# Second product turned round: w_out stationary, g moving in four 64x64 tiles, and a transpose of the output on VectorE

## Chip, cores, metric

One core of a Trainium2 chip. The metric is the device time of one execution in microseconds (us), on the slowest core (there is only one). "Before" and "changed" name the two kernels.

## The reference

```python
# a short causal convolution over the sequence, softmaxed weights per head, then a two-layer product
out = einsum('hk,bskhg->bshg', softmax(weight), windows_of(x))   # x: 8 x 4096 x 192, 8 heads, 7 taps
h = out.reshape(32768, 192) @ w_in                               # w_in: 192 x 2048
g = maximum(0.01 * h, h)
return g @ w_out                                                 # w_out: 2048 x 192, result fp32
```

Three parts share the work: VectorE does the convolution (y), TensorE the first product (h = y w_in), ScalarE the leaky ReLU on the way from PSUM to SBUF (g), TensorE the second product (g w_out).

## The kernel before

32 blocks of 2 x 512 tokens (two batch rows, index `e`). The first four blocks are worked in half groups of 256 tokens, to get going earlier; the other 28 are whole groups of 512. The second product of a group runs during the next group's first product, in "slots": a slot is the matmuls for one of the 16 pieces of 128 hidden channels.

The contraction of the first product is 192 = 3 x 64, so the array is split into two row tiles of 64 rows, one for each batch row:

```python
def mm1(grp, u):                       # one unit of the first product: 128 hidden channels
    ...
    for c in range(NCH):               # 3 pieces of the contraction
        for e in range(2):             # row tile = batch row
            ps = slice(e * CH, (e + 1) * CH)
            nc.tensor.matmul(out=ph[:, e, i * T : (i + 1) * T], lhsT=w_in_of(f, ps, c),
                             rhs=y[ps, c, t0 : t0 + T], start=(c == 0), stop=(c == NCH - 1))
    nc.scalar.activation(out=g[blk][...], in_=ph, func=Prelu, alpha=0.01)

def mm2_one(rt, m, fc, start, stop):   # second product: g stationary, w_out moves, 192 columns
    ...
    return nc.tensor.matmul(out=po[m], lhsT=g[b][ps, fc, e, s * 128 : (s + 1) * 128],
                            rhs=w_out[ps, fc, :], start=start, stop=stop)
```

The two row tiles each take half of a 128-long piece of the contraction, and the kernel keeps them out of one PSUM bank at the same time. So a pair of outputs is worked in two rounds (row tile 0 on output A and 1 on B, then the other way), with a "seal" between: a small ScalarE or VectorE instruction that waits for the last matmul of the round and is waited for by the first of the next.

```python
def mm2_slot(q):
    ...
    for rt in range(2):
        ins = mm2_one(rt, pair[rt ^ rnd], fc, first and rnd == 0, last and rnd == 1)
        if first and rnd == 1:
            sync(ins, seal, "both row tiles have left these banks")
    if last and rnd == 0:
        seal_round(p, ins)             # evacuates the previous pair's second output
    if last and rnd == 1:
        evac_o(pair[0])                # copy PSUM -> SBUF, 128 x 192, then a store
```

## Time and profile before

| | before |
|---|---|
| time, median of 3 | 692.45 us (691.92 to 692.78) |
| span of the profiled run | 690.8 us |
| TensorE, VectorE, ScalarE busy | 99%, 73%, 74% |
| output packets | 768 B each |

The three groups of the page that the change touches, besides those that the prediction shows. Columns: line, engine, operation, out<-in, sizes, count | busy us, mean ns of one | idle before it:

```profile
L429 PE MATMUL po<-w_out,g 64*128 64x192 bf16 (+1 forms) x8064 | 387.9, 243 | 0.0
L403 PE MATMUL ph<-yt,w_in 64*128 64x512 bf16 (+1 forms) x3456 | 384.1, 352 | 1.5 <-ACT g L410 0.7
...
L476 DVE COPY o_sb<-po 128x192 f32<-128x192 f32 x224 | 80.1, 358 | 163.9 <-PE po L429 156.3
```

The two products cost about the same. TensorE is hardly ever idle, while VectorE's copies wait for it.

### The profile page before, as it was taken

The page shows a single profiled execution, that of the slowest core. Times are in us where ns is not written, and L with a number is a line of the kernel's source. Part 1 is how long each engine was busy: PE and PEld are TensorE (multiplying, and loading weights), DVE is VectorE, ACT ScalarE, POOL GpSimd, SP SyncE. Part 2 cuts the span into 40 slices and gives each one's busy share as a digit, 9 for nine tenths or more (in the row PEclk, how much of TensorE's full clock was granted, in tenths as well). Part 3 has the DMA queues.
Part 4 walks back from the last instruction along what each step waited for, and adds up shares of the span by engine and source line. Part 5 has one row for each costly group of instructions (what it writes and reads, how often), then busy time and mean ns, then how long its engine had stood idle before and what let it go on. Part 6 is the DMA issues. An engine that isn't in the chain of part 4 may idle for free.

```text
span 690.8 us, 25914 instructions
## 1 busy us (share of the span) xinstructions
PE 685.2 (99%) x11708; PEld 584.0 (85%) x11708; DVE 501.6 (73%) x986; ACT 514.4 (74%) x569; POOL 148.0 (21%) x206
## 2 busy tenths in 40 slices
PE   9999999999999999999999999999999999999998
PEld 6999988888888888888888888888888888888887
DVE  5899666777777787777787777777777877777712
ACT  6888898777777777777777777777777777777771
POOL 6822222211222201222202222112222112000000
PEclk9999999999999999999999999999999999999999
DMA  9976656455565545565455566355565455322112
GB/s 151 117 93 94 82 69 84 80 78 70 75 85 82 76 77 75 66 94 82 71 78 71 74 84 88 67 78 75 77 82 80 77 75 66 67 60 59 48 42 64
DMA packets 184159, 53.79 MB, mean 78 GB/s; under 512 B 149104, under 2 KB 183664, under 8 KB 184048
## 3 DMA queue, kind: packets, MB, share of 16 engines
q0 software_dynamic: 99536, 14.76, 30.2%
q1 hardware_dynamic: 84512, 37.38, 22.8%
q8 instruction: 91, 1.49, 0.9%
q14 instruction: 20, 0.16, 0.1%
HBM read 29.88 MB, written 25.17 MB: 80 GB/s over the span
## 4 chain that ended last, share of the span: by engine, by line
PE 98%; ACT 2%; issue 0%; DVE 0%
PE po L429 49%; PE ph L403 47%; ACT g L410 2%; PE acc L212 1%; PE warm L284 1%; PE ptr L149 0%; ACT yt L371 0%; DVE o_sb L476 0%; PE ptr L156 0%; PE wps L320 0%; PE wps_l L320 0%; DVE zero L227 0%; DVE junk L229 0%
## 5 line engine op out<-in xcount | busy, mean ns | idle before, releaser
L410 ACT ACTIVATE g<-ph 128x1024 bf16<-128x1024 f32 x512 | 496.3, 1021 | 155.9 <-PE ph L403 155.4
L193 DVE SCALAR_TENSOR_TENSOR yt<-xt,wk,yt 128x512 bf16<-128x512 bf16 (+1 forms) x630 | 399.5, 691 | 0.2
L429 PEld LDWEIGHTS <-g 64*128 64x128 bf16 (+1 forms) x8064 | 361.9, 94 | 34.4 <-issue 0.2
L429 PE MATMUL po<-w_out,g 64*128 64x192 bf16 (+1 forms) x8064 | 387.9, 243 | 0.0
L403 PE MATMUL ph<-yt,w_in 64*128 64x512 bf16 (+1 forms) x3456 | 384.1, 352 | 1.5 <-ACT g L410 0.7
L403 PEld LDWEIGHTS <-w_in 64*128 64x128 bf16 x3456 | 226.0, 111 | 64.7 <-issue 3.7
L78 POOL DMA_DIRECT2D x_bf<-in_x_dram x180 | 134.6, 772 | 422.6 <-DMA xt<-x_bf 420.1
L476 DVE COPY o_sb<-po 128x192 f32<-128x192 f32 x224 | 80.1, 358 | 163.9 <-PE po L429 156.3
L187 DVE TENSOR_SCALAR yt<-xt,wk 128x512 bf16<-128x512 bf16 (+1 forms) x105 | 36.8, 381 | 12.8 <-DMA xt<-x_bf 12.6
L476 ACT COPY o_sb<-po 128x192 f32<-128x192 f32 x32 | 10.2, 320 | 1.5 <-PE po L429 0.2
L168 DVE COPY xt<-ptr 128x384 bf16<-128x384 bf16 x7 | 2.2, 354 | 6.9 <-PE ptr L156 4.5
L212 PE MATMUL acc<-xt,diag 64*64 64x256 bf16 x84 | 6.7, 327 | 0.0
L212 PEld LDWEIGHTS <-diag 64*64 64x64 bf16 x84 | 5.5, 133 | 1.3 <-DVE wk L366 0.4
L284 PE MATMUL warm<-zero 128*128 128x256 bf16 (+1 forms) x20 | 4.8, 405 | 1.1 <-DVE junk L229 1.1
L127 POOL DMA_DIRECT2D x_half<-in_x_dram x6 | 4.3, 714 | 3.2 <-DMA w_in<-in_moe_w_in_dram 3.2
L284 PEld LDWEIGHTS <-zero 128*128 128x128 bf16 x20 | 2.5, 136 | 2.1 <-DVE junk L229 1.1
L249 POOL DMA_DIRECT2D w_in<-in_moe_w_in_dram x6 | 3.9, 654 | 0.0
L371 ACT ACTIVATE yt<-acc,rsum 128x256 bf16<-128x256 f32 x3 | 1.4, 474 | 2.9 <-PE acc L212 2.9
L345 ACT ACTIVATE diag<-ident,whm 128x64 bf16<-128x64 bf16 x14 | 3.5, 335 | 0.0
L123 POOL DMA_DIRECT2D x_rows<-in_x_dram x4 | 2.9, 733 | 0.2 <-issue 0.2
L133 ACT CAST x_half<-x_nat 128x384 bf16<-128x384 f32 x2 | 1.0, 512 | 1.2 <-DMA x_nat<-in_x_dram 1.1
L290 ACT ACT_TABLE_LOAD x1 | 1.3, 1283 | 0.8 <-PEq L575 0.8
(37 smaller groups left out, 11.9 us busy)
## 6 DMA issues: line engine op xcount, KB each, us to landing
out_dram<-o_sb SPq DMA_DIRECT2D x117, 192.0 KB, 2.1
x_bf<-in_x_dram POOLq DMA_DIRECT2D x180, 64.0 KB, 3.2
out_dram<-o_sb SPq DMA_DIRECT2D x22, 96.0 KB, 1.6
xt<-x_bf SPq DMA_TRANSPOSE x90, 2.5
w_in<-in_moe_w_in_dram POOLq DMA_DIRECT2D x4, 192.0 KB, 5.8
w_in<-in_moe_w_in_dram POOLq DMA_DIRECT2D x2, 384.0 KB, 9.4
w_out<-in_moe_w_out_dram POOLq DMA_DIRECT2D x1, 768.0 KB, 11.2
x_nat<-in_x_dram SPq DMA_DIRECT2D x2, 192.0 KB, 2.6
```

The source lines that it names most:

```text
L78: nc.gpsimd.dma_start(out=t[:, c, :, e, :], in_=src[2 * rp + e, :, :, c * CH : (c + 1) * CH],)
L127: nc.gpsimd.dma_start(out=x_half[q][:, c, :, e, :], in_=rows[:, e, :, c * CH : (c + 1) * CH],)
L187: lambda s=src, d=dst, c=c: nc.vector.tensor_scalar_mul(d, s, wk[:, c, 0:1])
L193: lambda s=src, d=dst, c=c, k=k: nc.vector.scalar_tensor_tensor(out=d, in0=s, scalar=wk[:, c, k : k + 1], in1=d, op0=mybir.AluOpType.mult, ...
L212: lambda k=k, p=p, a=a, e=e, ps=ps: nc.tensor.matmul(out=acc[ps, :T], lhsT=diag[c][ps, p, k, :], rhs=xt[0][ps, c, a : a + T], start=(k == ...
L249: nc.gpsimd.dma_start(out=w_in[n][e * CH : (e + 1) * CH], in_=moe_w_in[:, fs].rearrange("(c p) f -> p c f", p=CH),)
L284: nc.tensor.matmul(out=wa[:, 0, 0:cols], lhsT=zero[:, 0:128], rhs=zero[:, 0:cols], start=True, stop=True,)
L345: nc.scalar.activation(out=diag[c][:, p, k, :], in_=ident2, func=mybir.ActivationFunctionType.Copy, scale=whm[:, c, p, k : k + 1],)
L403: nc.tensor.matmul(out=ph[:, e, i * T : (i + 1) * T], lhsT=w_in_of(f, ps, c), rhs=y[ps, c, t0 : t0 + T], start=(c == 0), stop=(c == NCH - 1),)
L410: act = nc.scalar.activation(out=g[blk][:, nf * u : nf * (u + 1), :, t0 : t0 + T], in_=ph.rearrange("p e (i t) -> p i e t", i=nf), func=my ...
L429: return nc.tensor.matmul(out=po[m], lhsT=g[b][ps, fc, e, s * 128 : (s + 1) * 128], rhs=w_out[ps, fc, :], start=start, stop=stop,)
L476: ins = copy(out=o_sb[:, n % 2, :], in_=po.pop(n))
```

## The change

The intent: let the second product stream as many columns per matmul as the first (512 instead of 192), so that a fixed cost per matmul is paid less often. For that w_out becomes stationary (64 x 64 pieces) and g moves. The output then comes out transposed, channels on the partitions. VectorE's 32x32 transpose turns it while evacuating, and stores write 384-byte runs. Both products use four 64x64 tiles from the second whole group on, so that TensorE stays in one mode (one shape of tile). Three outputs per group (192 = 3 x 64 channels) are worked in three rounds.

```diff
-    g_pool = ctx.enter_context(tc.tile_pool(name="g", bufs=3))
+    g_pool = ctx.enter_context(tc.tile_pool(name="g", bufs=2))
 ...  first product: each 64x128 tile in two 64x64 halves (M = 64)
+                    for m in range(0, 128, M):
+                        nc.tensor.matmul(
+                            out=ph[m : m + M, e, i * T : (i + 1) * T],
+                            lhsT=w_in_of(f, ps, c, m, m + M),
+                            rhs=y[ps, c, t0 : t0 + T], ...)
 ...  second product
+    def mm2_slot(q):
+        gi, fc = divmod(q, NR * NFC)               # NR = 3 rounds of NFC = 16 slots
+        rnd, fc = divmod(fc, NFC)
+        ...
+        for rt in range(2):
+            r = (rnd + rt) % NR
+            ps = slice(rt * CH, (rt + 1) * CH)
+            for e in range(2):
+                ins = nc.tensor.matmul(
+                    out=acc2[gi, r][e * CH : (e + 1) * CH, 0:T],
+                    lhsT=w_out[ps, fc, r::NR],
+                    rhs=g[b][ps, fc, e, t0 : t0 + T], ...)
+                if first and not fresh:
+                    sync(ins, seal, "the other row tile has left this bank")
+        if last and rnd < 2:
+            seal = nc.scalar.copy(out=junk, in_=junk)
+            sync(seal, ins, "between the rounds")
+        if last and rnd > 0:
+            for r in ((), (1,), (0, 2))[rnd]:
+                evac_t(gi, r)
+    def evac_t(gi, r):
+        nc.vector.transpose(out=osb[gi, 0][:, 0 : T // GB, :, r],
+            in_=acc2.pop((gi, r))[:, 0:T].rearrange("p (j k) -> p j k", k=GB))
+        ...  after r == 2: four stores, runs of 3 * 32 fp32 = 384 B
 ...  slots per step of a whole group
-        quota = plan.get(i, [(avail - slot) // steps] * steps)
+        quota = plan.get(i, [16] * 4 if T == HT else [5, 5, 6, 5, 5, 6, 8, 8])
```

The outputs of the half groups and of the last group are still made by the old second product. That of the last half group runs during the first whole group, so the new one begins one group later, with the first whole group's output: 27 groups in all.

More of the change, by code (lines that the diff above doesn't have):

```diff
@@ L46 @@
     NPEC = 2
+    GB = 32
+    NR = D // (2 * GB)
     const_pool = ctx.enter_context(tc.tile_pool(name="const", bufs=1))
@@ L252, in load_w_in, with w_in_of @@
         )
-    def w_in_of(f, ps, c):
+    def w_in_of(f, ps, c, m0, m1):
         n = max(n for n in range(3) if pieces[n] <= f)
         a = (f // RUN * RUN - pieces[n]) * 128 + f % RUN
-        return w_in[n][ps, c, a : a - f % RUN + RUN * 128 : RUN]
+        return w_in[n][ps, c, a + m0 * RUN : a - f % RUN + m1 * RUN : RUN]
     load_w_in(0, 0)
@@ L381, with mm1 @@
         evac_y(act_scale)
-    g, po, osb, seal = {}, {}, {}, None
+    g, po, acc2, osb, seal = {}, {}, {}, {}, None
+    NSW = 2 * NHALF
     subs = [
-        (b, e, t0 // 128 + s)
-        for b, t0, T in groups for e in range(2) for s in range(T // 128)
-    ]
-    NSUB = len(subs)
-    LAST = NSUB - 2 * SUB
-    SINGLE = LAST - 14
-    def mm1(grp, u):
+        (b, e, t0 // 128 + n)
+        for b, t0, T in groups[:NSW] for e in range(2) for n in range(T // 128)
+    ]
+    LAST = len(subs)
+    subs += [(NBLK - 1, e, n) for e in range(2) for n in range(SUB)]
+    def mm1(grp, u, M):
         blk, t0, T = grp
@@ L402, in mm1 @@
                     ps = slice(e * CH, (e + 1) * CH)
-                    nc.tensor.matmul(
-                        out=ph[:, e, i * T : (i + 1) * T],
-                        lhsT=w_in_of(f, ps, c),
-                        rhs=y[ps, c, t0 : t0 + T],
-                        start=(c == 0),
-                        stop=(c == NCH - 1),
-                    )
+                    for m in range(0, 128, M):
+                        nc.tensor.matmul(
+                            out=ph[m : m + M, e, i * T : (i + 1) * T],
+                            lhsT=w_in_of(f, ps, c, m, m + M),
+                            rhs=y[ps, c, t0 : t0 + T],
+                            start=(c == 0),
+                            stop=(c == NCH - 1),
+                        )
         act = nc.scalar.activation(
@@ L435, in mm2_one, with mm2_row_slot @@
         )
-    def mm2_slot(q):
+    def mm2_row_slot(q):
         p, fc = divmod(q, 2 * NFC)
@@ L467, in seal_round, with w_out_of @@
         sync(seal, ins, "between the rounds")
+    def w_out_of(ps, fc, r):
+        return w_out[ps, fc, r::NR]
+    def mm2_slot(q):
+        nonlocal seal
+        gi, fc = divmod(q, NR * NFC)
+        rnd, fc = divmod(fc, NFC)
+        first, last = fc == 0, fc == NFC - 1
+        if first:
+            for r in ((1, 0), (2,), ())[rnd]:
+                acc2[gi, r] = psum_o.tile([128, ST], FP32, name="acc2", tag="po")
+        for rt in range(2):
+            r = (rnd + rt) % NR
+            fresh = (rnd, rt) in ((0, 0), (0, 1), (1, 1))
+            done = (rnd, rt) in ((1, 0), (2, 0), (2, 1))
+            b, t0, T = groups[gi]
+            ps = slice(rt * CH, (rt + 1) * CH)
+            for e in range(2):
+                ins = nc.tensor.matmul(
+                    out=acc2[gi, r][e * CH : (e + 1) * CH, 0:T],
+                    lhsT=w_out_of(ps, fc, r),
+                    rhs=g[b][ps, fc, e, t0 : t0 + T],
+                    start=first and fresh,
+                    stop=last and done,
+                )
+                if first and not fresh:
[7 more added lines that the diff above has]
+    def evac_t(gi, r):
+        b, t0, T = groups[gi]
+        if (gi, 0) not in osb:
+            osb[gi, 0] = o_pool.tile([128, ST // GB, GB, NR], FP32, name="o_t")
+        nc.vector.transpose(
+            out=osb[gi, 0][:, 0 : T // GB, :, r],
+            in_=acc2.pop((gi, r))[:, 0:T].rearrange("p (j k) -> p j k", k=GB),
+        )
+        if r != 2:
+            return
+        rp, st = divmod(b, NB)
+        t = osb.pop((gi, 0))
+        for e in range(2):
+            rows = out_rows[2 * rp + e, st * ST + t0 : st * ST + t0 + T, :].rearrange(
+                "(j k) d -> k j d", k=GB
+            )
+            for h in range(2):
+                p = (2 * e + h) * GB
+                nc.sync.dma_start(
+                    out=rows[:, :, h * NR * GB : (h + 1) * NR * GB],
+                    in_=t[p : p + GB, 0 : T // GB].rearrange("p j k r -> p j (k r)"),
+                )
     def evac_o(n):
@@ L471, in evac_o @@
         rp, st = divmod(b, NB)
-        if n % 2 == 0 or n >= SINGLE:
-            osb[n // 2] = o_pool.tile([128, 2, D], FP32, name="o_sb")
-        o_sb = osb[n // 2]
+        if n % 2 == 0 or n >= LAST:
+            osb[n] = o_pool.tile([128, 2, D], FP32, name="o_sb")
+        o_sb = osb[n if n >= LAST else n - n % 2]
         copy = nc.scalar.copy if b < NHALF else nc.vector.tensor_copy
         ins = copy(out=o_sb[:, n % 2, :], in_=po.pop(n))
-        if n >= SINGLE:
+        if n >= LAST:
             t0 = st * ST + s * 128
-            nc.sync.dma_start(
-                out=out_rows[2 * rp + e, t0 : t0 + 128, :], in_=osb.pop(n // 2)[:, n % 2, :]
-            )
+            nc.sync.dma_start(out=out_rows[2 * rp + e, t0 : t0 + 128, :], in_=o_sb[:, n % 2, :])
         elif n % 2 == 1:
@@ L485, in evac_o @@
                 out=out_rows[2 * rp + e, t0 : t0 + 256, :].rearrange("(c p) d -> p c d", p=128),
-                in_=osb.pop(n // 2),
+                in_=o_sb,
             )
@@ L493 @@
     plan = {
-        2 * NHALF - 2: [16, 8, 8, 16],
-        2 * NHALF - 1: [8, 8, 16, 16],
-        2 * NHALF: [16, 8, 8, 16, 8, 8, 16, 16],
+        0: [0] * 4,
+        NSW - 2: [16, 8, 8, 16],
+        NSW - 1: [8, 8, 16, 16],
+        NSW: [16, 8, 8, 16, 8, 8, 16, 16],
     }
-    slot, avail = 0, 0
+    slot = 0
     for i, grp in enumerate(groups):
@@ L512 @@
             for u in range(2 * j, 2 * j + 2):
-                mm1(grp, u)
+                mm1(grp, u, 128 if i <= NSW else CH)
                 if i == 0 and u == 1:
@@ L537 @@
             for _ in range(quota[j]):
-                mm2_slot(slot)
+                if i <= NSW:
+                    mm2_row_slot(slot)
+                else:
+                    mm2_slot(slot)
                 slot += 1
@@ L549 @@
             last_half = t0 + T == ST
+            if i == NSW and j == steps - 1:
+                evac_o(LAST - 1)
+                slot = NSW * NR * NFC
             if j == steps // 4 and last_half:
@@ L553 @@
                 transpose_x(blk + 2)
-        avail += 2 * T // 128 * NFC
-    evac_o(LAST - 1)
-    for n in range(LAST, NSUB):
+    for n in range(LAST, len(subs)):
         po[n] = psum_o.tile([128, D], FP32, name="po", tag="po")
```

## The prediction

> **What bounds the kernel now.** I read the page's busy line and chain first: is one engine the whole time, and does anything release it?
>
> ```profile
> PE 685.2 (99%) x11708; PEld 584.0 (85%) x11708; DVE 501.6 (73%) x986; ACT 514.4 (74%) x569; POOL 148.0 (21%) x206
> ...
> PEclk9999999999999999999999999999999999999999
> ...
> PE 98%; ACT 2%; issue 0%; DVE 0%
> ```
>
> TensorE is busy for 99% of the span at full clock, and 98% of the chain that ended last is TensorE following itself. So only what shortens TensorE's own stream, or newly stalls it, can move the time. Next, the chain in order of time over one whole group in the steady part (324.15 to 345.07 us), of which I show two of the eight steps:
>
> ```profile
> 324.15 1.29 PE ph L403 x12
> 325.45 1.32 PE po L429 x32
> 326.77 1.29 PE ph L403 x12
> 328.06 1.32 PE po L429 x32
> ```
>
> L403 is the first product (w_in stationary), L429 the second (g stationary, w_out moving). A step is 12 + 32 matmuls with nothing between. In the whole group TensorE has no gap: 20.92 us. Full speed of the columns alone: 6 x 512 + 16 x 192 columns per row tile per step at 2.4 columns per ns are 1.280 + 1.280 us; eight steps are 20.48 us. So the reserve in one whole group is 0.44 us, or 2.1%; over the 27 groups that the change touches 11.9 us, 1.7% of the run. That caps the gain **below 2%** before any detail.
>
> The start times of single matmuls in the trace show what the 0.44 us are: pairs of L403 (512 columns, one in each row tile) follow each other every 215.8 ns, where the columns take 213.3; pairs of L429 (192 columns) every 82.5, where they take 80.0. Each matmul of a row tile costs 2.5 ns over its columns, whatever its length: 48 + 128 matmuls per row tile and group x 2.5 ns = 0.44 us. The mean durations on the page (243 and 376 ns) contain the pipeline and are not the pitch.
>
> The other engines, in the waits from 100 to 670 us and VectorE's order of time:
>
> ```profile
> ACT g L410 <- PE ph L403: 144.1, 215, 0.7
> DVE o_sb L476 <- PE po L429: 142.0, 208, 2.3
> ...
> 394.80 0.36 DVE L476 COPY o_sb<-po 128x192 f32<-128x192 f32 x1 [0.27 <-PE po L429]
> 395.07 2.07 DVE L193 SCALAR_TENSOR_TENSOR yt<-xt,wk,yt 128x512 bf16<-128x512 bf16 x3
> ```
>
> Both wait for TensorE, never the other way round: they have slack, VectorE 5.3 us of each 20.9 (15.58 busy).
>
> **What the Trainium skill says.** (1) "TensorE: Matmul & The Clock Gate", section Back-to-back issue gap, gives N/2.4 + 2.5 ns for warm matmuls; this trace agrees exactly for row tiles (215.8 at 512, 82.5 at 192). (2) "TensorEngine Tiling (Array Packing)", section Tiling Modes: 64x64 mode is four independent tiles, and changing the mode drains the array. The second is presumably why the first product is also cut into 64x64 tiles: both products stay in one mode. The trace has one short stretch in which all four tiles are used, the start-up transposes of L156:
>
> ```profile
> L156 PEld LDWEIGHTS <-x_rows x48: 103/110/110, 13.4 to 20.2; 64*64 64x64 bf16 x48
> L156 PE MATMUL ptr<-ident,x_rows x48: 192/193/213, 13.4 to 20.2; 64*64 64x64 bf16 x48
> ...
> 20.03 0.38 PE L156 MATMUL ptr<-ident,x_rows 64*64 64x64 bf16 x24
> ```
>
> Columns: least/median/most ns; then start, length. 24 matmuls in 0.38 us, of which 0.19 is the last one's latency: so four run side by side, and by their start times (3 to 4 ns apart within four, then a new four each 31.5 ns) they really are independent. Weight loads keep that pace too, though each shows 103 to 110 ns. (3) "Vector Engine (DVE) Microarchitecture Reference", section 3.8, says that the 32x32 transpose sustains one element per cycle per lane; there is no such transpose in this trace to check it. (4) "DMA: Bandwidth & Descriptors", Specifications: transfers below 512 B fall under line rate. The trace has 768 B output packets at 39 ns on average, and 256 B ones in the same queue at 23, so small packets do cost more per byte.
>
> **The change, part by part**, per whole group.
>
> Removed: 256 L429 matmuls of 192 columns. Two row tiles, so 128 x 82.5 ns = 10.56 us. Added: 48 slots of four matmuls of 512 columns. If four tiles pitch like the pairs, 48 x 215.8 = 10.36 us. Moved: the first product is 192 instead of 96 matmuls, but on four tiles instead of two, so 48 x 215.8 = 10.36 us both before and after. Sum: 20.72 instead of 20.92, **0.20 us saved**, times 27 groups = 5.4 us.
>
> The doubt is the pitch of a four. In the L156 stretch a four of 64 columns took 31.5 ns, 4.8 over its 26.7; pairs of 64-column transposes in L149 took 29.2, 2.5 over. If the extra 2.3 ns is the price of four tiles, each of the 96 fours per group takes 218.1, the group 20.94 us, and the gain is gone (-0.5 us over the run). But the L156 loads are as frequent as the matmuls, and load and matmul may limit each other there, while at 512 columns a load has 216 ns to hide in. A two-tile 64x64 stream exists as well (L212, 256 columns): a pair each 108.4 ns, 1.7 over. I choose 216.5 as the middle: 96 x 216.5 = 20.78, 0.14 saved, **3.8 us** in all.
>
> VectorE: removed 8 copies x 0.358 = 2.86 us; added 3 transposes of 128x512. Estimate: the 192-column copy's 358 ns are 200 ns at one element per cycle of the skill's 0.96 GHz plus 158 fixed; 512 give 533 + 158 = 0.69 us, three 2.07. VectorE is relieved by 0.8 us. Their place matters more: one comes after round 2 (two thirds through), two after the group's end. After the first, VectorE must still do six convolution steps (6 x 0.69 = 4.1 us) before the next group starts. Slots 5,5,6,5,5,6,8,8 put the end of round 2 at 14.68 us; 14.9 + 0.69 + 4.1 = 19.7 < 20.72. It holds until a transpose takes 1.5 us.
>
> ScalarE: two small copies more per group as seals, some 0.2 us each, 15.5 of 20.7 busy. In a step with 5 slots the period falls from 2.61 to 1.295 + 1.08 = 2.37 us. ScalarE's two activations end 2.82 us after the step's first matmul (309.15 + 1.94 against 308.27); the second first-product unit of the next step needs that buffer at 2.37 + 0.65 = 3.02. Slack 0.2 us: thin, but there. A seal has the 1.3 us of two first-product units to come in.
>
> DMA: output goes from 1024 packets of 768 B to 2048 of 384 B. At an estimated 35 ns (between the 23 of 256 B and the 39 of 768 B) that is 4.5 instead of 2.5 us of 16 engines per group: the share rises from 0.57 in that group to about 0.67. Off the path: nothing waits for it but the output tiles, of which there are four.
>
> Not changed: the half groups (first 100 us), the last group in its old form (12.0 us on the chain), and the last stores. One more change of mode costs perhaps 0.2 us once.
>
> So 692.45 - 3.8 + 0.2 = 688.9 us.
>
> **The rivals.** *The four-tile stream is dearer than I think*: nothing in the trace shows four full-length streams together with different moving data in the two column tiles. For it: the 4.8 ns above. Against it: that figure is tiny. At 4.8 the time is 693; if unhidden loads add 10 ns to each four, 27 x 96 x 10 ns = 26 us more, 715. *A new wait takes the place*: ScalarE's 0.2 us of slack missing by 0.1 in four steps per group would cost 11 us (about 700); a transpose of over 1.5 us would stall TensorE at each group's start (2 us each: +14). Against: the margins computed above. *DMA becomes the bound*: the small packets delay the x transposes. VectorE waited for those 12.6 us in all already, without TensorE noticing; I see up to 3 us here. *More gain than thought*: with the fixed cost vanishing wholly in four tiles, 20.48 per group, 680.9; not 2% even so.
>
> **Range and chances.** Mostly a size between 686.9 (pitch 215.8) and 693 (218.1), with a tail for new waits: 685 to 697. Faster by over 2% (below 678.6) lies beyond full array speed: 0.02. Slower by over 2% (above 706.3) needs 0.5 us in each group, from a stall or from exposed loads: 0.08. Within 2%: 0.90.
>
> **What would show it.** A whole group of 20.7 to 20.8 us in the chain; fours 215 to 217 ns apart; TensorE still 98% of the chain; transposes of 0.65 to 0.75 us; VectorE's busy time down by some 20 us; packets up by 27,600. Wrong if TensorE waits for ScalarE in the five-slot steps, for VectorE at each group's start, or if its matmuls, without any wait, come further apart than 218 ns.

## The result

The changed kernel took 687.4 us (687.14 to 687.94, 4 runs), the kernel before 692.62 beside it. The ratio is 0.9927 (95% interval 0.991 to 0.9944). A second set (below) gave 0.9932. A ratio here is the mean time of one kernel's fast runs over that of the other's of the same rounds, so not quite the ratio of the medians that I quote.

The changed kernel's page, busy line, chain and the groups that answer to those shown of before:

```profile
PE 679.2 (99%) x12572; PEld 466.0 (68%) x12572; DVE 483.7 (71%) x851; ACT 524.6 (77%) x623; POOL 147.5 (22%) x206
...
q8 instruction: 98, 1.61, 0.9%
...
PE 95%; DMA 2%; POOL 1%; ACT 1%; issue 0%; DVE 0%; POOLq 0%
...
L406 PE MATMUL ph<-yt,w_in 64*64 64x512 bf16 (+2 forms) x6048 | 377.9, 363 | 1.4 <-ACT g L413 0.7
L495 PE MATMUL acc<-g,w_out 64*64 64x512 bf16 x5184 | 316.5, 376 | 0.0
...
L517 DVE STREAM_TRANSPOSE o_t<-acc 128x512 f32<-128x512 f32 x81 | 68.1, 884 | 170.0 <-PE acc L495 170.0
```

And the chain in order of time, three steps of a whole group:

```profile
326.30 1.29 PE ph L406 x24
327.59 1.08 PE acc L495 x20
328.67 1.29 PE ph L406 x24
329.96 1.08 PE acc L495 x20
331.04 1.29 PE ph L406 x24
332.34 1.29 PE acc L495 x24
```

A step of the first product still takes 1.29 us, now with 24 matmuls instead of 12. Twenty second-product matmuls (5 slots) take 1.08 us. Nothing lies between. By the start times of single matmuls, a four (one matmul on each of the four tiles) follows a four every 215.83 ns in both products: 512 columns at 2.4 per ns plus 2.5 ns. (The traces give the 2.4 themselves: 512 columns take 133.3 ns longer than the 192 of the kernel before.) This start-to-start time is called the pitch below. Corresponding points of two groups lie 20.72 us apart, where it was 20.92. The saving, 0.20 us in each of 27 groups, is 5.4 us; measured were 5.2 and (second set) 4.4 us.

Most of the 5% of the chain that is not TensorE's lies at the very start, where this run's first second-product matmul waited 0.2 us for the w_out load and the chain followed that load back. The 1% of ScalarE is four stretches of 1.95 us between 77 and 105 us; the kernel before has such stretches there too. In the steady part the chain is all TensorE.

### The profile page after: what moved, and what is told of

The parts are those of the page before. It is cut to its first block, busy times and chain, and to the rows that moved or that the text cites. A ratio compares the mean times of both kernels' runs of the same rounds, so it can differ in the third digit from the quotient of the medians.

```text
span 685.2 us, 27404 instructions
## 1 busy us (share of the span) xinstructions
PE 679.2 (99%) x12572; PEld 466.0 (68%) x12572; DVE 483.7 (71%) x851; ACT 524.6 (77%) x623; POOL 147.5 (22%) x206
## 4 chain that ended last, share of the span: by engine, by line
PE 95%; DMA 2%; POOL 1%; ACT 1%; issue 0%; DVE 0%; POOLq 0%
PE ph L406 47%; PE acc L495 41%; PE po L432 7%; DMA w_out<-in_moe_w_out_dram 2%; ACT g L413 1%; POOL w_in L251 1%; POOL x_rows L125 0%; POOL sel L236 0%; DVE o_sb L543 0%; POOL ident masks.py:199 0%; POOL sel L234 0%; POOL ident masks.py:197 0%; PE ptr L151 0%; POOLq masks.py:199 0%; POOLq L642 0%
## 5 line engine op out<-in xcount | busy, mean ns | idle before, releaser
L195 DVE SCALAR_TENSOR_TENSOR yt<-xt,wk,yt 128x512 bf16<-128x512 bf16 (+1 forms) x630 | 388.2, 696 | 0.2
L406 PE MATMUL ph<-yt,w_in 64*64 64x512 bf16 (+2 forms) x6048 | 377.9, 363 | 1.4 <-ACT g L413 0.7
L495 PE MATMUL acc<-g,w_out 64*64 64x512 bf16 x5184 | 316.5, 376 | 0.0
L406 PEld LDWEIGHTS <-w_in 64*64 64x64 bf16 (+1 forms) x6048 | 237.7, 129 | 98.9 <-issue 3.9
L495 PEld LDWEIGHTS <-w_out 64*64 64x64 bf16 x5184 | 166.3, 118 | 110.5
L517 DVE STREAM_TRANSPOSE o_t<-acc 128x512 f32<-128x512 f32 x81 | 68.1, 884 | 170.0 <-PE acc L495 170.0
L432 PE MATMUL po<-w_out,g 64*128 64x192 bf16 (+1 forms) x1152 | 59.7, 243 | 0.2 <-DMA w_out<-in_moe_w_out_dram 0.2
L432 PEld LDWEIGHTS <-g 64*128 64x128 bf16 (+1 forms) x1152 | 55.2, 94 | 2.0 <-issue 0.8
L505 ACT COPY junk<-junk 128x1 f32<-128x1 f32 x54 | 10.3, 191 | 3.9
L543 DVE COPY o_sb<-po 128x192 f32<-128x192 f32 x8 | 2.8, 356 | 6.8 <-PE po L432 3.8
```

Source lines behind the costliest of these rows:

```text
L195: lambda s=src, d=dst, c=c, k=k: nc.vector.scalar_tensor_tensor(out=d, in0=s, scalar=wk[:, c, k : k + 1], in1=d, op0=mybir.AluOpType.mult, ...
L406: nc.tensor.matmul(out=ph[m : m + M, e, i * T : (i + 1) * T], lhsT=w_in_of(f, ps, c, m, m + M), rhs=y[ps, c, t0 : t0 + T], start=(c == 0), ...
L495: ins = nc.tensor.matmul(out=acc2[gi, r][e * CH : (e + 1) * CH, 0:T], lhsT=w_out_of(ps, fc, r), rhs=g[b][ps, fc, e, t0 : t0 + T], start=fi ...
L505: seal = nc.scalar.copy(out=junk, in_=junk)
L517: nc.vector.transpose(out=osb[gi, 0][:, 0 : T // GB, :, r], in_=acc2.pop((gi, r))[:, 0:T].rearrange("p (j k) -> p j k", k=GB),)
L543: ins = copy(out=o_sb[:, n % 2, :], in_=po.pop(n))
```

## The experiments

Twelve kernels ran; all but the one marked gave correct results. Summary first (medians; ratio to the kernel before):

| run | what is different from the changed kernel | us | ratio |
|---|---|---|---|
| after_again | nothing | 687.74 | 0.9932 |
| old_form_64 | second product as before (192 columns, 2 rounds), but both products in 64x64 tiles | 706.98 | 1.0224 |
| cols_256 | 512 columns in two matmuls | 690.68 | 0.9975 |
| cols_mix | in two or three, alternately | 692.82 | 1.001 |
| cols_192 | in three | 729.51 | 1.0529 |
| cols_128 | in four | 857.49 | 1.2379 |
| first_uncut | first product in 64x128 tiles | 744.63 | 1.0753 |
| even_slots | six slots in each step | 743.48 | 1.0738 |
| extra_mid | two more transposes after round 2 | 700.07 | 1.0111 |
| extra_end | two more transposes at the group's end | 688.51 | 0.9947 |
| half_stores | half of the stores left out (wrong result) | 687.86 | 0.9937 |
| two_half | two blocks in half groups, not four | 691.19 | 0.9975 |

### Is it the fixed cost per matmul? after_again, old_form_64, cols_256, cols_128

My theory: the gain is 2.5 ns per matmul of a tile, times fewer matmuls. Rivals: four tiles are the gain in themselves; or something else of the change is (VectorE's relief, the seals).

> The changed kernel again, as the yardstick of the three runs beside it: a ratio of 0.991 to 0.994 to the kernel before, some 687.4 us, and fours of matmuls 215.8 ns apart.

> The kernel before, with both products cut to 64x64 tiles from the second whole group on, but g still stationary and w_out moving in 192 columns. Theory (the gain is the 2.5 ns that each matmul of a tile costs over its columns, times the fewer matmuls): a tile still gets 128 matmuls of 192 columns and 48 of 512 per group, so a group stays at 20.92 us and the time at 692.5 us (+-1). Rival A (four tiles side by side are the gain, whatever streams): near 687 us. Rival B (four tiles cost 4.8 ns instead of 2.5 for short columns, as the start-up transposes hinted): 128 x 2.3 ns x 27 = 8 us more, 700 us.

```diff
 # on the kernel before: the first product cut as in the change, and the second
-        return nc.tensor.matmul(out=po[m], lhsT=g[b][ps, fc, e, s * 128 : (s + 1) * 128], ...)
+        return [nc.tensor.matmul(out=po[m][k : k + M],
+                    lhsT=g[b][ps, fc, e, s * 128 + k : s * 128 + k + M], ...)
+                for k in range(0, 128, M)]         # M = 64 from the second whole group on
```

> The changed kernel with the 512 columns of g in two matmuls of 256, in all but the first and last slot of each round (42 of 48 slots). Theory: 42 fours more per group x 2.5 ns x 27 groups = 2.8 us over the changed kernel, some 690.2 us. Rival (the gain comes from VectorE's relief, fewer seals or fewer buffers): no change, 687.4 us.

> The same in four matmuls of 128 columns. Theory: 126 fours more per group x 2.5 ns x 27 = 8.5 us, some 695.9 us; with the 4.8 ns of the start-up transposes for each short four, 168 x 2.3 ns x 27 = 10.4 us on top, 706 us. Rival: no change, 687.4 us.

```diff
-                    out=acc2[gi, r][e * CH : (e + 1) * CH, 0:T],
-                    rhs=g[b][ps, fc, e, t0 : t0 + T],
+                    out=acc2[gi, r][e * CH : (e + 1) * CH, lo:hi],   # 128 or 256 columns each,
+                    rhs=g[b][ps, fc, e, t0 + lo : t0 + hi],          # whole in first and last slot
```

(The first and last slots of a round stay whole because the check before the chip refuses a version that cuts them: a matmul that opens an accumulation, in a bank where another is still open.)

Measured: the yardstick 687.74. cols_256 took 690.68, **2.9 us** more where the theory said 2.8 and the rivals 0. That is the clean confirmation: nothing else of the change differs. The fours of 256 columns start 109.2 ns apart, 106.7 + 2.5.

old_form_64 took 707.0, which **none** of the three had said. Its matmuls are not slow: a four of 192 columns follows a four every 82.5 ns (median), exactly as the pairs of the kernel before. So rival A (four tiles gain by themselves) is out, and so is rival B (4.8 ns for short columns). The time went elsewhere. And cols_128, at 857.5 instead of 696, lost 160 us although its fours, too, start 55.8 ns apart (53.3 + 2.5) as long as they run. TensorE's order of time, first old_form_64, then cols_128 (start, length, then the group, count and idle time before):

```profile
310.47 1.53 PE L431 MATMUL po<-w_out,g 64*64 64x192 bf16 x58
312.69 0.35 PE L431 MATMUL po<-w_out,g 64*64 64x192 bf16 x6 [0.69 <-issue]
```

```profile
325.02 0.87 PE L406 MATMUL ph<-yt,w_in 64*64 64x512 bf16 x12
326.94 0.87 PE L406 MATMUL ph<-yt,w_in 64*64 64x512 bf16 x10 [1.06 <-issue]
327.43 2.15 PE L507 MATMUL acc<-g,w_out 64*64 64x128 bf16 x116
329.25 0.38 PE L406 MATMUL ph<-yt,w_in 64*64 64x512 bf16 x2
330.69 1.51 PE L406 MATMUL ph<-yt,w_in 64*64 64x512 bf16 x22 [1.06 <-issue]
```

The pauses have no releaser ("issue"), and fall in the midst of a run of like matmuls, in the first product as well as in the second. I numbered TensorE's matmuls and loads through the whole run: between 100 and 650 us, after **all 22** pauses of old_form_64 and **all 122** of cols_128 (a pause: starts over 330 ns apart; one at the first whole group, which every kernel of the table below has, is left out), TensorE begins again at the same number modulo 256. And the page's queue 8 moves instructions, 16 KB at a time:

```profile
PE 691.5 (98%) x21212; PEld 638.9 (91%) x21212; DVE 501.2 (71%) x986; ACT 514.6 (73%) x569; POOL 147.5 (21%) x206
...
q8 instruction: 165, 2.70, 1.7%
```

```profile
q8 instruction: 204, 3.34, 1.6%
```

2 x 21212 instructions in blocks of 256 are 165.7 blocks (old_form_64); cols_128 has 52360, 204.5 blocks; the changed kernel 25144, 98.2 blocks. So each packet holds 256 TensorE instructions of 64 B, and the pauses stand at one place relative to the blocks. In cols_128 and old_form_64 a new block begins every 3.9 us on average, and both run at the same 65.3 and 65.6 instructions per us; so the new theory: **TensorE's supply of instructions** ends there.

### Is it the supply of instructions? cols_mix, cols_192

> Test of why four tiles with short matmuls lost so much. In the two kernels that did (128 columns; the old form in 64x64), TensorE's pauses all begin anew at the same instruction number modulo 256, and both run at 65.3 to 65.6 TensorE instructions per us, one instruction block of 16 KB (256 instructions) each 3.9 us; the kernel with 256 columns has 53.0 per us and no such pause. Theory: the supply of instructions ends at some 65.5 per us. This kernel cuts the 512 columns into three (192, 192, 128) in half of the 42 slots and into two in the other half: 159 fours, 1272 instructions per group, 60.9 per us, below the limit. Expected: 63 fours more than the changed kernel x 2.5 ns x 27 = 4.3 us, 691.7 us, no pauses. Rival (short matmuls on four tiles are slow in themselves, below some length): a third of the way to the kernel with 128 columns, tens of us more.

> Three matmuls (192, 192, 128) in all 42 slots: 180 fours, 1440 instructions per group, which the matmuls alone would take in 20.93 us (68.8 per us). Theory: supply of 65.5 per us makes it 21.98 us, so 84 x 2.5 ns x 27 + 27 x 1.05 = 34 us over the changed kernel, 721 us, with pauses at one instruction number modulo 256. Without a limit of supply: 693.1 us. Rival (short matmuls are slow in themselves): about half way to the kernel with 128 columns, 770 us.

```diff
+                cuts = [(0, 192), (192, 384), (384, T)]               # cols_192: always
+                # cols_mix: that for even fc, [(0, 256), (256, T)] for odd fc
```

TensorE instructions per us between 150 and 600 us, the pauses, and the time beyond the changed kernel that the 2.5 ns do not explain (median less 687.6, less the fours added x 2.5 ns x 27):

| kernel | instructions per us | pauses | unexplained us |
|---|---|---|---|
| before | 33.7 | 0 | |
| changed | 37.1 | 0 | |
| cols_256 | 53.0 | 0 | 0.2 |
| cols_mix | 60.8 | 2 | 1.0 |
| cols_192 | 64.1 | 52 | 36.2 |
| cols_128 | 65.3 | 122 | 161.4 |
| old_form_64 (against the kernel before) | 65.6 | 22 | 14.9 |

Half of cols_mix's slots hold the same three short matmuls as cols_192, yet it loses 1 us instead of 36; the rival that short matmuls are slow in themselves foretold a third of cols_128's loss. All 52 and both 2 pauses stand at the same number modulo 256 as before. The size of cols_192 was off: 729.5 instead of 721, since it got 64.1 and not 65.5 per us; the limit is not one exact number.

The traces tie the pauses to the packets more closely. Each of the 198 pauses (2, 52, 122 and 22) ends 1.2 to 1.6 us (median 1.4) after a packet of queue 8 has landed, and always at the same instruction counted from that packet, 256 per packet. In none of the seven kernels does that instruction start sooner than 1.19 us after its packet's landing. In the kernels without a pause it comes later: at the earliest 1.6 us after in cols_256, 3.4 in the changed kernel and 5.3 in the kernel before. No two of these packets overlap in time. So a block's time divides as follows in cols_128 (medians): 1.1 us for the packet, 1.4 from its landing to the end of the pause, 1.2 until the next packet starts, 3.7 together, where pauses of successive blocks end 3.75 apart. Why the next packet starts no sooner, and what fills the 1.4 us, no run here shows; that stays open.

### Why is the first product cut too? first_uncut

The drain that this expectation speaks of is the one of the page that the prediction names (Tiling Modes). The run measures what a change of mode costs, not the drain as such.

> The first product stays in 64x128 tiles, the second in four 64x64. Theory: the mode changes 16 times in each of 27 groups, 432 times, and each change drains the array: the last matmul's latency beyond its columns is 163 ns by the profile (376 - 213), so up to 70 us more, 757 us; if a change is cheap (20 ns), 9 us more, 696. Rival (a change of mode between these two costs nothing, the cut is needless): 687.4.

```diff
-                mm1(grp, u, 128 if i <= NSW else CH)
+                mm1(grp, u, 128)
```

744.63 us, 57 more: 132 ns for each of the 432 changes of mode, at the upper end of what I expected. Its page and chain:

```profile
PE 736.7 (99%) x9980; PEld 389.3 (52%) x9980; DVE 482.6 (65%) x851; ACT 524.7 (71%) x623; POOL 147.0 (20%) x206
```

```profile
327.21 1.22 PE acc L495 x20
328.43 1.42 PE ph L406 x12
```

1.22 and 1.42 us for what takes 1.08 and 1.29 in the changed kernel. TensorE still shows as 99% busy, so the cost is no idle time on the page; only the pitch reveals it. From the start of the last matmul of one product to the start of the first of the other it is 306 ns, in the changed kernel 206. So the cut of the first product, which by itself saves nothing, is what makes the change possible at all.

### Do the seals hide? even_slots

> Six slots in each of the eight steps, so that the rounds end inside a step (after 4 and after 2 slots of one) and the seal is no longer covered by two units of the first product. Theory: at each of the two seals per group TensorE waits for the round's last matmul to drain, for ScalarE to finish its two activations (2.82 us after the step began, where the 4 slots are through after 2.16) and for the 0.19 us copy: 0.5 to 0.9 us each, 27 to 49 us in all, 715 to 736 us. Rival (even steps suit ScalarE better and the seal is hidden by queued work): same or faster.

```diff
-        quota = plan.get(i, [16] * 4 if T == HT else [5, 5, 6, 5, 5, 6, 8, 8])
+        quota = plan.get(i, [16] * 4 if T == HT else [6] * 8)
```

743.48 us, 56 more, a little over the range that I gave. TensorE and then ScalarE around the second seal of a group (two slots into the step that begins at 331.03):

```profile
332.32 0.60 PE L495 MATMUL acc<-g,w_out 64*64 64x512 bf16 x8
333.97 1.07 PE L495 MATMUL acc<-g,w_out 64*64 64x512 bf16 x16 [1.04 <-ACT junk L505]
```

```profile
331.90 1.94 ACT L413 ACTIVATE g<-ph 128x1024 bf16<-128x1024 f32 x2 [0.65 <-PE ph L406]
333.72 0.19 ACT L505 COPY junk<-junk 128x1 f32<-128x1 f32 x1
```

The two slots were through at 332.75; the next matmul started at 333.97, because the seal sits behind two activations in ScalarE's order. From the step starts, the seal after four slots costs 0.80 us and this one 1.25, 2.05 us per group, 55 in 27. The uneven 5, 5, 6, 5, 5, 6, 8, 8 is therefore no matter of taste: it puts each round's end at a step's end, and the seals behind 1.29 us of other work.

### Does VectorE's added work lie beside TensorE's? extra_mid, extra_end

> The transpose after the second round is done three times (same data, same place). A transpose took 0.893 us in the changed kernel, 0.8 when one follows another, so VectorE starts the last six convolution steps 1.6 us later. In the profile they ended at 338.45 us and TensorE began the next group at 339.51, so 1.06 us of slack: a stall of 0.5 to 0.6 us in each of 26 groups, 13 to 16 us, some 702 us, with TensorE waiting for VectorE's convolution. Rival (only VectorE's busy share counts, 71% and then 78%): no change, 687.4.

> The same two extra transposes per group, but of the last tile at the group's end. Same busy time of VectorE as extra_mid. There VectorE has some 4 us of idle time before it next waits for TensorE, so no change: 687.4 us (+-1). If it is busy time that counts, the same as extra_mid.

```diff
+        src = acc2.pop((gi, r))[:, 0:T].rearrange("p (j k) -> p j k", k=GB)
+        for _ in range(3 if r == 1 else 1):       # extra_mid; extra_end: r == 2
+            nc.vector.transpose(out=osb[gi, 0][:, 0 : T // GB, :, r], in_=src)
```

Same instructions, same number, another place: 700.07 and 688.51 us. extra_end lies 0.9 us over the yardstick by medians taken in different calls; its ratio of 0.9947 (0.9932 to 0.9962) contains the yardstick's 0.9932 just so. In the steady part its trace shows no loss: the groups lie 20.72 us apart, as in the changed kernel. At the very end it shows one: the last matmul ends at 681.8 us (681.9 in the changed kernel), but VectorE waits there 4.75 us for an output tile instead of 2.80, and its last copy ends 0.7 us later. In extra_mid VectorE's and then TensorE's order of time show why:

```profile
338.81 2.75 DVE L519 STREAM_TRANSPOSE o_t<-acc 128x512 f32<-128x512 f32 x3 [4.39 <-PE acc L495]
341.43 4.00 DVE L195 SCALAR_TENSOR_TENSOR yt<-xt,wk,yt 128x512 bf16<-128x512 bf16 x6
```

```profile
344.60 0.67 PE L406 MATMUL ph<-yt,w_in 64*64 64x512 bf16 x8
345.49 1.09 PE L406 MATMUL ph<-yt,w_in 64*64 64x512 bf16 x16 [0.22 <-DVE yt L195]
```

VectorE stood idle for 4.39 us, then did three transposes and the six convolution steps that the next group needs. TensorE started on the two pieces of y that were ready (8 matmuls), could have gone on at 345.03, and went on at 345.49, when the last piece was done: 0.46 us, in 26 groups 12 us. (I had expected 0.5 to 0.6 and forgot the 0.43 us of those eight matmuls, but also took a repeated transpose for 0.8 us where it is 0.9: each begins only when the one before has ended.) In the changed kernel the convolution is through 1.06 us before the group begins:

```profile
333.67 0.90 DVE L517 STREAM_TRANSPOSE o_t<-acc 128x512 f32<-128x512 f32 x1 [4.39 <-PE acc L495]
334.45 4.00 DVE L195 SCALAR_TENSOR_TENSOR yt<-xt,wk,yt 128x512 bf16<-128x512 bf16 x6
```

### Do the small stores matter? half_stores

> Wrong on purpose: two of the four stores of each whole group are left out (from the second whole group to the last but one), so that half of the small output packets are gone. Theory: the stores are off the path, no change, 687.4 us (+-0.7). Rival (packets of 384 B, or their reads from the output tile, slow the engines down and ate a part of the gain): 1 to 3 us faster.

```diff
-            for h in range(2):
+            for h in range(1):                    # wrong on purpose: half of the output stays unwritten
```

687.86 us, ratio 0.9937: no change, with 10.6 MB less written. The stores are off the path.

### A faster version? two_half

> An attempt at a faster version: only two blocks instead of four in half groups at the start. Each of the two blocks freed goes from 64 + 64 pairs of 256 columns and old second product (8 x 2.63 = 21.0 us, plus shares of the 0.25 us stalls in steps of 8 slots) to 20.72 us. Theory: 0.6 us faster, some 686.8 us, if the loads of x keep up at the start; if they don't, some us slower, with VectorE waiting for the transposed x.

```diff
-    NHALF = 4
+    NHALF = 2
```

691.19 us (688.94 to 692.09), 3.5 slower than the changed kernel. Its chain at the start runs through the loads and then VectorE, not TensorE:

```profile
40.26 2.44 DMA xt<-x_bf
42.70 0.02 issue
42.72 0.35 DVE yt L189
43.08 11.93 DVE yt L195 x18
55.01 0.04 issue
55.06 1.17 PE ph L406 x8
```

The first whole group, moved forward, needs all its 512 tokens convolved when x has only just come in. TensorE waits 1.8 us for VectorE there. Just after it, the granted clock of the profiled run is 0.83 on average between 50 and 60 us, some 1.7 us more (10 us x 0.17; the 32 matmuls of L432 that begin at 56.23 take 2.56 us in the chain, where 32 take 1.32 otherwise). Of the six executions the one with a mean clock of 1.0 took 688.94 us; the five of 0.997 and 0.998 took 690.54 to 692.09. So about half of the loss is the wait and half the lower clock; that the wait caused the lower clock is not shown. The half groups are worth their cost. No run beat the changed kernel.

## Why the prediction was right

Predicted 688.9 us (685 to 697), within 2%; measured 687.4. The mechanism was right: less fixed cost per matmul, and no new wait in the steady part. To stay within 2% alone says little, for a change worth nothing would have done that too. What was tested is the group's 20.72 us and the terms below.

- **The cap.** The reserve of 0.44 us per group was read rightly: the group went from 20.92 to 20.72, and no version came near 20.48.
- **Second product, 10.56 to 10.36 us; first product unchanged.** The sum with the pairs' pitch was right to the digit, but it was not the one that was put forward (next point). cols_256 shows that the fixed 2.5 ns per matmul is the cause.
- **The pitch of a four**, the term that I mis-sized: I chose 216.5 ns as a middle between 215.8 and 218.1, because start-up transposes of 64 columns took 4.8 ns over their columns. The other start-up stretch that I read, L212, is not so even either: its quickest pairs start 108 to 110 ns apart, as I took it, but many 112 to 113. The pitch is 215.83, and 2.5 over at 256, 192 and 128 columns too. The 4.8 ns of the transposes did not carry over. That makes 5.4 instead of 3.8 us of gain. Why the transposes took 4.8 is open.
- **VectorE**, the other term that was mis-sized: a transpose takes 0.89 us alone, and two that follow one another hold VectorE for 1.50 us (1.63 to the end of the second), not 0.69 each. (The 0.96 GHz of that estimate stands in the Trainium skill's "VectorE: DVE Perf Modes", Specifications, which the prediction did not name; with one size of transpose no run checks the rate of one element per cycle.) It is still under the 1.5 us that I gave as the limit, and its busy time fell by 17.9 us, where I said some 20. extra_mid shows that there is a limit, but it lies higher. My own sum gives 20.72 - 14.9 - 4.1 = 1.7 us. By the traces it is near 2.3: the 0.78 us for which a transpose holds VectorE, 1.06 of slack, and the 0.43 of the eight matmuls that do not need the last piece.
- **ScalarE, the thin slack of 0.2 us.** It held: the waits of the changed kernel list 0.7 us for TensorE on ScalarE, as before. ("Never the other way round" holds for the steady part; the chain's ScalarE stretches between 77 and 105 us, in both kernels, lie before it.) In the order of time ScalarE's two activations end at 331.31 us, and TensorE's second unit of the next step begins at 331.52: 0.2 us, as computed. even_slots shows what badly placed seals cost; it does not measure this slack.
- **DMA.** Packets rose by 27,540 (I said 27,600), a packet of 384 B took 28.6 ns on average where I estimated 35, and a store took 4.6 us to land instead of 2.1; off the path, as half_stores shows.
- **Change of mode.** Foreseen as the reason for cutting the first product; first_uncut puts 57 us on it.
- **Chain 98% TensorE**: 95% on the page, for the start-up reason told above; in the steady part all of it.
- **A slip without effect:** at the full speed of the columns the sum is 692.45 - 11.9 = 680.6 us (680.8 with the added 0.2), not 680.9.

One rival of mine, "unhidden loads", had a neighbour that I did not see: not the loads' time, but the mere number of instructions. The changed kernel has 37 TensorE instructions per us and is far from the limit near 65. Had the change shortened the matmuls instead of lengthening them, it would have run into it.

## What to carry to other kernels

When TensorE is on the chain all the time, look at the pitch of its matmuls, not at busy shares: what is over the columns (here 2.5 ns per matmul and tile) is all that a rearrangement of the same columns can win, and it caps the gain before anything is built. Exchange the operands so that the longer side moves, keep all products in one tiling mode, put each engine's new work where that engine is idle before its next deadline, and count TensorE's instructions per us when you cut matmuls into smaller ones.

## What the Trainium skill lacked or had wrong

- "Runtime: NRT & Kernel Launch", Instruction fetch mechanics, has the 16 KiB blocks of 256 instructions and calls the cost of crossing into the next one mostly hidden. It gives no rate at which TensorE outruns them. Here it did: 52 to 122 pauses at 64.1 and 65.3 instructions (loads and matmuls together) per us, 22 at 65.6, always at one place of a block, which lengthened a run by up to 161 us; at 53.0 there were none and at 60.8 two.
- "TensorEngine Tiling (Array Packing)", Tiling Modes, says that a change of mode drains TensorE but gives no cost: 132 ns per change here (57 us over 432), between 64x128 and 64x64.
- The same page, Restrictions, says that column tiling disables fast weight load. It does not say what that costs. No cost is seen in the pitch here: with four 64x64 loads per four matmuls it was N/2.4 + 2.5 ns down to 128 columns (55.8 ns), outside the pauses.
- "TensorE: Matmul & The Clock Gate", Back-to-back issue gap, gives 131 ns per matmul of 512 columns as the sustained figure for a stream of load and matmul pairs, and N/2.4 + 2.5 only for isolated ones. In these streams each tile took 215.8 ns, the second formula.
- "VectorE: DVE Perf Modes", The three transpose paths, has a 128x128 bf16 transpose on VectorE (311 ns) but none of fp32 from PSUM: 128x512 took 0.89 us here, and two that followed one another 1.63.
